# Hypermixer after linear attention: output columns written in token order with one store a tile, and one pool of eight PSUM banks

## The chip, the cores and the metric

The kernel runs on one core of one Trainium2 chip. The metric is the device time of the whole program in microseconds (us), lower is better. Before the change it took 134.56 us (median of three runs, 133.71 to 135.49). Each kernel also has one execution under the hardware profiler; "span" is the length of that execution, about 1.8 us shorter than the time the same run is booked with. On one core a run is called slow when it is over 1.5% above the fastest run of the same kernel.

Engines in the profile: PE is TensorE's matmul, PEld its weight load, DVE VectorE, ACT ScalarE, POOL GpSimd, SP SyncE, which issues most of the DMAs. A name with q (SPq, ACTq) is that engine's instruction queue.

## The reference, cut to what matters

```python
# attention: q, k, v are (8 batches, 8 heads, 576 tokens, 64), fp32
q_p = phi(q); k_p = phi(k)              # relu, times cos and sin of the position
kv  = einsum('bhsf,bhsd->bhfd', k_p, v); z = sum(k_p, axis=2)
attn = (q_p @ kv) / (q_p . z + 1e-6)
x = attn as (8, 576, 512)
# hypermixer: token mixing whose weights are made from x itself
wq = x @ w_q; wk = x @ w_k              # 512 -> 64
W  = einsum('bsd,btd->bst', wq, wk) / 8
mixed = einsum('bst,btd->bsd', W, x)
out = relu(mixed) @ w_out               # (8, 576, 512) fp32
```

The kernel never forms W: it computes kx = wk^T x (64 x 512) and then mixed^T = kx^T wq^T. 28.3 MB of q, k and v come in and 9.44 MB go out.

## The kernel before

A sequence of 576 tokens is cut as token = 9 p + c, with p from 0 to 63 and c from 0 to 8. On the chip a batch's tokens stand in the order (c, p), so a run of 64 columns holds tokens 9 apart. `mix_sb` holds relu(mixed)^T for two batches, bf16, 512 features on partitions (four groups of 128) by 2 x 576 token columns. Its columns are the weights of the last matmul, so their order is the order of the output's rows.

```python
CS = ((0, 5), (5, C9))                 # C9 = 9;  hs = 288, S = 576, D = 64
K0, N0, M0, M1, M2, M3 = 0, 2, 4, 5, 6, 7    # PSUM banks: qT and kv own 0-1, num owns 2-3

def mx_mm(b, j, m):                    # mixed^T: half the columns, two groups of features
    nh, i = divmod(j, 2)
    for r in range(2):
        rhs = (wT_bufs[b % 2][0:64, D + nh * hs:D + (nh + 1) * hs] if r == 0
               else wqTs[b][64:128, nh * hs:(nh + 1) * hs])
        nc.tensor.matmul(bank(m + r)[:, 0, 0:hs],
                         kxs[b][half_rows(r), i * P:(i + 1) * P], rhs, start=True, stop=True)

def mx_evac(b, j, m, eng):             # PSUM fp32 -> SBUF bf16, with relu and scale
    ...
    c0 = (b % 2) * S + nh * hs
    dst = mixs[b // 2].rearrange("p (r i) n -> p r i n", r=2)[:, :, i, c0:c0 + hs]
    src = bank(m, 2)[:, :, 0:hs]
    if eng is nc.scalar: nc.scalar.activation(dst, src, AF.Relu, scale=scale_moe)
    else: eng.tensor_scalar(dst, src, scale_moe, 0.0, op0=ALU.mult, op1=ALU.max)

def wout_mm(bp, rt, m):                # one output tile: 128 columns of mix_sb
    for dmc in range(NDM):
        nc.tensor.matmul(bank(m)[:, 0, :], mixs[bp][:, dmc, rt * P:(rt + 1) * P],
                         wo_sb[:, dmc, :], start=(dmc == 0), stop=(dmc == NDM - 1))

def store(bp, rt, qs):                 # two halves of 64 rows, 9 rows apart in DRAM
    for hi in range(2):
        qs[hi].dma_start(
            dataclasses.replace(out, offset=out.offset + out_dest(bp, rt, hi),
                                ap=[[C9 * DM, 64], [1, DM]]),
            o_sbs[bp, rt][64 * hi:64 * hi + 64, :])
```

A scheduler in the kernel (`plan_order`) fixes the order of all pieces and the engine of each evacuation beforehand. It simulates the engines with a table of times for each piece and picks the piece that can start first, less a weight for its priority. A half batch is called H (0 to 15). Names that occur below: qT, kv, num, norm, xT are attention's pieces for one H; wqk, wk, kx and mx make the mix for one batch; wo is an output tile. In the old scheduler mx, wo and the pieces before mx share banks 4 to 7.

## Time and profile before

| | before |
|---|---|
| time, median (range) | 134.56 us (133.71 to 135.49) |
| span of the profiled run, mean granted clock | 130.8 us, 0.974 |
| busy: PE, DVE, ACT, POOL | 105.8, 93.8, 78.5, 76.8 us |
| of PE's busy time, warm-up matmuls | 9.4 us |
| evacuation of mix: 24 on ACT, 8 on DVE | 657 and 756 ns each |
| last v cast; start of the last half batch's K-V product (kv.15) | 96.93; 105.15 us |

The two groups that the change touches most, from the table of the costliest groups. The columns are line, engine, operation, output and input with shapes and types, count; then busy us in all and mean ns of one; then the engine's idle time just before them and what ended it:

```profile
L520 ACT ACTIVATE mix_sb<-ps 128x576 bf16<-128x576 f32 x24 | 14.7, 657 | 2.4 <-PE ps L508 2.4
...
L522 DVE TENSOR_SCALAR mix_sb<-ps 128x576 bf16<-128x576 f32 x8 | 6.0, 756 | 4.0 <-PE ps L508 4.0
```

### The profile page before, as it was taken

To read this page: it belongs to the slowest core of one execution; us is meant where nothing else is said; L and a number is where in the kernel's file an instruction comes from. 1 tells how busy PE (TensorE), PEld (TensorE's weight loads), DVE (VectorE), ACT (ScalarE), POOL (GpSimd) and SP (SyncE) were. 2 spreads that over 40 slices of the span, in tenths; PEclk is the share of its full clock that TensorE was granted. 3 is DMA by queue.
4 is the path that set the end of the run, shared out by engine and by line. 5 is a ranking of instruction groups with operands and counts; after the bars stand their busy time and mean duration, and the time that the engine had idled before them with its cause. 6 is when DMAs were issued, how large, how long until landed. Compare 5 with 4: busy or idle time off the path is not lost.

```text
span 130.8 us, 5363 instructions
## 1 busy us (share of the span) xinstructions
PE 105.8 (81%) x2279; PEld 61.8 (47%) x2279; DVE 93.8 (72%) x153; ACT 78.5 (60%) x154; POOL 76.8 (59%) x121
## 2 busy tenths in 40 slices
PE   5947685885699989986999699889947999899930
PEld 2325253563546546643756366556624664443300
DVE  1065979689994999959999987989659876346200
ACT  6950063658756796639557595787637865655440
POOL 7728988896779999975697876885371000000000
PEclk9999999999959999999999999999999999999995
DMA  3999999999999999999999999999974034837973
GB/s 88 369 383 394 345 310 403 394 388 390 389 393 388 374 391 396 401 378 376 316 393 413 368 359 378 383 373 295 382 214 87 5 80 89 177 75 167 211 226 110
DMA packets 21239, 39.40 MB, mean 301 GB/s; under 512 B 3040, under 2 KB 4576, under 8 KB 21216
## 3 DMA queue, kind: packets, MB, share of 16 engines
q1 hardware_dynamic: 20544, 38.08, 85.0%
q10 hardware_dynamic: 672, 0.98, 2.5%
q8 instruction: 18, 0.29, 0.9%
q14 instruction: 5, 0.04, 0.1%
HBM read 29.62 MB, written 9.44 MB: 299 GB/s over the span
## 4 chain that ended last, share of the span: by engine, by line
PE 43%; DMA 23%; DVE 14%; ACT 5%; POOL 5%; issue 4%; SPq 2%; ACTq 1%; POOLq 0%
PE ps L532 19%; DMA raw<-in_k_dram 12%; DMA raw<-in_q_dram 9%; PE ps L422 5%; PE ps L462 5%; PE ps L397 5%; DVE kp L361 4%; DVE qpt_buf L389 4%; PE ps L492 3%; POOL rk L348 3%; PE ps L447 2%; PE ps L383 2%; DVE x_sb L435 2%; PE ps L508 2%; POOL rq_buf L348 2%
## 5 line engine op out<-in xcount | busy, mean ns | idle before, releaser
L532 PE MATMUL ps<-wo_sb,mix_sb 128*128 128x512 bf16 x144 | 37.3, 386 | 2.0 <-issue 1.7
L348 POOL TENSOR_SCALAR rq_buf<-raw 128x640 bf16<-128x640 f32 (+1 forms) x32 | 26.2, 835 | 9.3 <-DMA raw<-in_q_dram 7.9
L373 POOL TENSOR_SCALAR v_buf<-raw 128x640 bf16<-128x640 f32 (+1 forms) x30 | 27.1, 920 | 7.4 <-DMA raw<-in_v_dram 6.6
L361 DVE TENSOR_TENSOR kp<-rk,cossin 128x2304 bf16<-128x2304 bf16 (+2 forms) x17 | 22.5, 1324 | 11.3 <-ACT rk L346 6.1
L335 ACT COPY o_sb<-ps 128x512 f32<-128x512 f32 x32 | 18.8, 586 | 15.8 <-PE ps L532 12.9
L435 DVE TENSOR_TENSOR x_sb<-ps,rec 128x640 bf16<-128x640 f32 x32 | 26.4, 824 | 1.1
L389 DVE TENSOR_TENSOR qpt_buf<-ps,cst 128x1152 bf16<-128x1152 bf16 x32 | 22.6, 747 | 0.0
L348 POOL TENSOR_SCALAR rk<-raw 128x640 bf16<-128x640 f32 (+1 forms) x30 | 19.5, 669 | 4.2 <-DMA raw<-in_k_dram 2.7
L422 PEld LDWEIGHTS <-qpt_buf 64*128 64x128 bf16 x640 | 14.3, 95 | 14.0 <-issue 13.2
L422 PE MATMUL ps<-kv_sb,qpt_buf 64*128 64x65 bf16 x320 | 16.3, 193 | 4.2 <-DVE x_sb L435 3.7
L532 PEld LDWEIGHTS <-mix_sb 128*128 128x128 bf16 x144 | 11.9, 98 | 15.6 <-issue 4.1
L335 ACT COPY xT_buf<-ps 128x640 bf16<-128x640 bf16 (+1 forms) x25 | 15.7, 650 | 3.0 <-PE ps L447 1.7
L422 PE MATMUL ps<-kv_sh,qpt_buf 64*128 64x65 bf16 x320 | 16.3, 192 | 1.1 <-issue 0.2
L397 PE MATMUL ps<-v_buf,kp 64*128 64x65 bf16 x576 | 13.1, 190 | 3.8 <-DVE qpt_buf L389 2.9
L520 ACT ACTIVATE mix_sb<-ps 128x576 bf16<-128x576 f32 x24 | 14.7, 657 | 2.4 <-PE ps L508 2.4
L397 PEld LDWEIGHTS <-kp 64*128 64x128 bf16 x576 | 10.6, 94 | 8.2 <-issue 3.4
L335 ACT CAST kv_sb<-ps 128x260 bf16<-128x260 f32 x13 | 4.9, 378 | 12.4 <-PE ps L397 12.2
L508 PE MATMUL ps<-wT_buf,kx 64*128 64x288 bf16 x32 | 8.5, 292 | 2.6 <-ACT mix_sb L520 1.9
L258 PE MATMUL ps<-warm 128*128 128x512 bf16 x31 | 9.4, 441 | 1.5 <-DVE warm L254 1.5
L383 PE MATMUL ps<-ident,rq_buf 64*128 64x64 bf16 x288 | 8.1, 192 | 2.6 <-POOL rq_buf L348 1.3
L433 DVE RECIPROCAL rec<-ps 128x10 f32<-128x10 f32 x32 | 6.8, 213 | 4.0 <-PE ps L426 3.8
L462 PE MATMUL ps<-xT_buf,wqk_sb 128*128 128x288 bf16 x64 | 9.2, 287 | 0.0
(51 smaller groups left out, 115.8 us busy)
## 6 DMA issues: line engine op xcount, KB each, us to landing
raw<-in_q_dram SPq DMA_DIRECT2D x15, 576.0 KB, 7.1
raw<-in_k_dram SPq DMA_DIRECT2D x15, 576.0 KB, 7.3
raw<-in_v_dram SPq DMA_DIRECT2D x15, 576.0 KB, 7.2
out_dram<-o_sb SPq DMA_DIRECT2D x67, 128.0 KB, 5.3
wo_f<-in_moe_w_out_dram SPq DMA_DIRECT2D x1, 1024.0 KB, 10.2
out_dram<-o_sb ACTq DMA_DIRECT2D x5, 128.0 KB, 2.9
raw<-in_k_dram ACTq DMA_DIRECT2D x1, 320.0 KB, 4.5
raw<-in_q_dram SPq DMA_DIRECT2D x1, 320.0 KB, 4.2
```

What stands on the lines that cost most here:

```text
L335: nc.scalar.copy(dst, src)
L348: eng.tensor_scalar(dst, src, FMAX, 0.0, op0=ALU.min, op1=ALU.max)
L361: nc.vector.tensor_mul(kp[H][:, 2 * lo:2 * hi], rks[H][:, lo:hi].rearrange("p c i d -> p (c i) d").unsqueeze(2) .to_broadcast([P, 2 * (hi ...
L373: eng.tensor_scalar(dst, src, 1.0, 1.0, op0=ALU.mult, op1=ALU.mult)
L389: nc.vector.tensor_mul(qpt_bufs[H % 2][:, r, :, D:SLOTS * D], bank_h(K0 + r)[:, 0:1, 0:HC].to_broadcast([P, 2, HC]), cst)
L397: nc.tensor.matmul(bank(K0 + r)[:, 0, i * (D + 1):(i + 1) * (D + 1)], kp[H][half_rows(r), 2 * c + i, :, :], v_bufs[H % 3][half_rows(r), c, ...
L422: nc.tensor.matmul(nb[t][:, u, :], qpt_bufs[H % 2][rows, r, w, u * P:(u + 1) * P], mv, start=(u == 0 and w == 0), stop=False)
L435: nc.vector.tensor_tensor(xv[:, h, r], nv[:, :, :, 0:D], rec.to_broadcast([P, 2, SC, D]), op=ALU.mult)
L462: nc.tensor.matmul(bank(m + nh)[:, 0, 0:hs], wqk_sb[:, dmc, :, :], xT_bufs[b % 2][:, dmc, nh * hs:(nh + 1) * hs], start=(dmc == 0), stop=( ...
L508: nc.tensor.matmul(bank(m + r)[:, 0, 0:hs], kxs[b][half_rows(r), i * P:(i + 1) * P], rhs, start=True, stop=True)
L520: nc.scalar.activation(dst, src, AF.Relu, scale=scale_moe)
L532: nc.tensor.matmul(bank(m)[:, 0, :], mixs[bp][:, dmc, rt * P:(rt + 1) * P], wo_sb[:, dmc, :], start=(dmc == 0), stop=(dmc == NDM - 1))
```

## The change

The intent is fourfold. Output tiles become 128 consecutive rows, so one store over 128 partitions replaces two over 64. For that, the evacuation of the mix writes each column to its token's place. The scheduler gives all eight PSUM banks to all pieces from one pool instead of reserving four of them. And its table of times is replaced by one said to come from a trace. The core of the diff:

```diff
 def mx_mm(b, j, m):
     nh, i = divmod(j, 2)
+    lo, hi = CS[nh]                    # halves of 320 and 256 columns, whole values of c
     ...
 def mx_evac(b, j, m, eng):
-        c0 = (b % 2) * S + nh * hs
-        dst = mixs[b // 2].rearrange("p (r i) n -> p r i n", r=2)[:, :, i, c0:c0 + hs]
-        src = bank(m, 2)[:, :, 0:hs]
+        c0 = (b % 2) * S
+        dst = (mixs[b // 2].rearrange("p (r i) n -> p r i n", r=2)[:, :, i, c0:c0 + S]
+               .rearrange("p r (s c) -> p r c s", c=C9)[:, :, lo:hi, :])
+        src = (bank(m, 2)[:, :, 0:(hi - lo) * D]
+               .rearrange("p r (c s) -> p r c s", c=hi - lo))
     ...
-    def store(bp, rt, qs):
-        for hi in range(2):
-            qs[hi].dma_start(...)      # as above
+    rows = out.rearrange("b s d -> (b s) d")
+    def store(bp, rt, eng):
+        r0 = 2 * bp * S + P * rt
+        eng.dma_start(rows[r0:r0 + P, :], o_sbs[bp, rt])
     ...
     # plan_order: times, priorities, dependencies, and banks
-        op(("qT", H), {"PE": .27}, [ago(H, "rq", H), ago(H, "kve", H - 1)], pa, "row")
+        op(("qT", H), {"PE": .26}, [ago(H, "rq", H), ago(H, "kv", H - 1),
+                                    ago(H > 1, "num", H - 2, 1)], pa, "row", 2)
-            op(("mxe", b, j), {"ACT": .67, "DVE": .76}, [("mx", b, j)], par["pme"], ...)
+            op(("mxe", b, j), {"ACT": .56, "DVE": .71}, [("mx", b, j)], par["pme"], ...)
-                        u = min((0, 2), key=lambda i: max(bank[i], bank[i + 1]))
+                        u = min((0, 2, 4, 6), key=lambda i: max(bank[i], bank[i + 1]))
     ... # likewise kv, num, norm, xT, wqk, kx, wo; a model of fetch pauses on PE
```

In the new `dst` the innermost index is p, and one step of it is 9 bf16 elements, 18 bytes.

## The prediction

> **What bounds the kernel now**
>
> I read the page's slices first, then busy time by stage, the waits, what the DMA engines moved in two short stretches, and the end of the chain of waits. From the slices (3.27 us each; busy in tenths):
>
> ```profile
> PE   5947685885699989986999699889947999899930
> DMA  3999999999999999999999999999974034837973
> GB/s 88 369 383 394 345 310 403 394 388 390 389 393 388 374 391 396 401 378 376 316 393 413 368 359 378 383 373 295 382 214 87 5 80 89 177 75 167 211 226 110
> ```
>
> The DMA engines are full until 98 us and then nearly idle, while PE works on to 125.5. So there are two limits in a row: inputs until 98 us, then whatever PE has not done yet. The table by stage puts numbers on it (columns: length, busy time of each engine, granted clock, DMA share, GB/s):
>
> ```profile
> 7.00:20.00 13.00, 8.93 (x216) 5.12 (x217) 9.60 (x17) 3.69 (x9) 9.56 (x12) 1.00 1.06 359
> 20.00:34.00 14.00, 9.57 (x304) 6.80 (x305) 12.19 (x20) 8.52 (x19) 11.45 (x16) 1.00 1.05 393
> 34.00:50.00 16.00, 14.73 (x318) 8.72 (x310) 13.73 (x21) 11.07 (x25) 14.52 (x20) 0.89 1.05 387
> 50.00:66.00 16.00, 14.29 (x351) 9.04 (x351) 13.90 (x24) 9.71 (x19) 12.30 (x15) 1.00 1.03 373
> 66.00:82.00 16.00, 14.59 (x367) 8.89 (x366) 14.32 (x25) 11.01 (x22) 12.45 (x18) 1.00 1.03 381
> 82.00:98.00 16.00, 13.37 (x340) 8.42 (x337) 12.68 (x22) 10.93 (x25) 10.82 (x14) 1.00 0.95 330
> 98.00:105.15 7.15, 6.02 (x166) 3.97 (x162) 6.44 (x12) 5.19 (x11) 0.71 (x2) 1.00 0.20 43
> 105.15:125.50 20.35, 19.46 (x223) 9.07 (x222) 9.80 (x18) 11.97 (x22) 0.00 (x0) 1.00 0.64 142
> 125.50:130.80 5.30, 0.00 (x0) 0.00 (x0) 0.00 (x0) 0.69 (x2) 0.00 (x0) 0.69 0.52 154
> ```
>
> I cut at 105.15 because there the K-V product of the last half batch (kv.15) starts. POOL casts its v from 96.93 to 98.71, so the input was ready 6.4 us before PE came to it. Then PE is 96% busy for 20.35 us, and 5.3 us follow the last matmul. So the end is: when PE reaches kv.15, plus 20.35, plus 5.3. From 34 us to kv.15 PE is idle 71.15 - (14.73 + 14.29 + 14.59 + 13.37 + 6.02) = 8.15 us, and from 7 to 34 us 27 - 18.50 = 8.5 us. That idle time is what a new schedule can win. The waits name it:
>
> ```profile
> PE ps L422 <- DVE x_sb L435: 3.7, 6, 1.1
> PE ps L397 <- DVE qpt_buf L389: 2.9, 8, 0.5
> PE ps L508 <- ACT mix_sb L520: 1.9, 4, 1.1
> PE ps L532 <- issue: 1.7, 1, 1.7
> ```
>
> Three of the four are waits for a PSUM bank: num for the norm that empties banks 2-3, kv for the q evacuation that empties banks 0-1, mx for an evacuation in the pool of four. Together 8.5 us over the run, 4.9 of it before 34 us.
>
> **What the Trainium skill says**
>
> "SBUF — State Buffer", section "Door 1: The DMA port swizzle": DMA bandwidth depends on how many of the 16 SBUF ports the partitions reach, and 64 consecutive partitions reach 8. The kernel stores each output tile as two halves of 64 partitions. The trace agrees. Loads alone at 24-38 us run at 391 GB/s. Around 62-64 us, where two tiles' halves are in the queue, the rate drops to 150-292 while the engines stay busy, and in the drain from 120 to 126 us, with stores alone, it is 214:
>
> ```profile
> DMA packets 2547, 5.47 MB, mean 391 GB/s; under 512 B 132, under 2 KB 132, under 8 KB 2544
> ...
> DMA packets 780, 1.28 MB, mean 214 GB/s; under 512 B 161, under 2 KB 161, under 8 KB 779
> ```
>
> "Runtime: NRT & Kernel Launch", section "Instruction fetch mechanics": instructions come in 16 KiB blocks of 256, and the cost is "mostly hidden". The trace has 18 packets and 0.29 MB on the instruction queue, which fits the block size; hidden is only partly true: PE's one long "issue" wait, 1.7 us before 97.1, has no other releaser, and I take it for a fetch behind the full queue.
>
> "VectorE: DVE Perf Modes", section "Why PSUM operands drop a tier": an fp32 PSUM operand caps the op at 1×, so the mix evacuation has no fast mode to lose by a strided output. The trace agrees: 756 ns for 576 elements. The SBUF page's note on 16-byte cachelines in the same Door 1 section says bf16 can stride for free up to 8 elements; the new writes step by 9 elements (18 bytes). No run here shows yet what that costs.
>
> **The change, part by part**
>
> *Stores.* The mix evacuation now writes columns in token order, so an output tile is 128 consecutive rows and 36 stores of 256 KB over 128 partitions replace 72 of 128 KB over 64. Bytes stay. What the half rate cost before the last load: from 34 to 98 us the four stages fall 3, 17, 9 and 60 GB/s short of 390, which is 16 x (3 + 17 + 9 + 60)/390 = 3.65 us. About 1.3 of that is the stretch 96.5-98 where no load is left, so 2.4 us. The order of DMA issues also puts 17 instead of 18 tiles ahead of the last v load: 0.26 MB / 390 GB/s = 0.7 us. The last v is cast about 3 us earlier, at 95.7 instead of 98.7. This is permission for PE, not yet gain. It also halves SP's store issues (0.547 us each, 36 fewer) and the number of DMAs in flight that must retire before the next issue.
>
> *Banks.* qT, kv and num no longer own fixed pairs. In the new order kv.0 stands before the q evacuation, and kv.15 no longer needs qe.15 out of its banks. On DVE, qe.14 and both norms of 13 now stand before mk.15; before, they stood behind it, so H = 14 hung back to kv.14 at 99.92. Before 34 us I expect 1.5 of the 4.9 us of bank waits back (the rest is data that is not there yet, and the output weights' 1 MB now load two halves earlier, ahead of q.3). Between 34 us and kv.15 I expect 3.5 of the 8.15 us back. So kv.15 moves from 105.15 to about 100.2, 4.4 us after its input is ready: PE's own work is then the limit, not the inputs.
>
> *PE work.* The same: 36 output tiles (144 matmuls at 386 ns), 32 num, 32 mx. I counted the new order after kv.15: 13 output tiles, as before. So the 20.35 us stay, except that kx.6 and kx.7 now have their evacuations (372 ns, with semaphores about 0.5 us) uncovered before mx.6.0 and mx.7.0: +1.0 us. The 12 more warm-up matmuls (30 against 18 beside the opening 13) stand in gaps and cost nothing.
>
> *The end.* The chain of waits for the last tiles:
>
> ```profile
> 121.35 2.36 DMA out_dram<-o_sb
> ...
> 123.81 0.59 ACT o_sb L335
> ...
> 125.63 0.47 ACTq L542
> ...
> 126.20 0.58 ACT o_sb L335
> ```
>
> ACT issues half of every late store between two evacuations: 0.59 + 0.47 and gaps, about 1.2 us a tile against PE's 0.97. It also waits for an output buffer that a slow store holds. The last evacuation so starts at 126.20, 0.7 us after its matmul. Now ACT issues only tiles 5 and 7 and stores drain at twice the rate: I take off 0.7 us here and 0.5 us of the 4.0 us from the last evacuation to the end.
>
> *Sum.* -1.5 - 3.5 + 1.0 - 1.2 = -5.2 us: a span of 125.6. The profiled span is 130.8 where the median time is 134.56; in the same ratio that is 134.56 x 125.6/130.8 = 129.2. Because PE at this density meets fetch stalls that I cannot place, I add 0.4: 129.6 us.
>
> **Rivals**
>
> *PE stays late.* PE has about 96 us of its own work (105.8 busy less 9.4 warm-up). If the idle time is mostly fetch and dependencies rather than banks, it moves and does not shrink. For it: the 1.7 us issue wait, and more instructions than before (4584 rows against 4560). Then only the end and about 1.5 us come off: 132 us.
>
> *The strided write costs.* If an 18-byte step adds a third to 32 mix evacuations (ACT 657 ns, DVE 756), that is 0.23 x 32 = 7 us spread over two engines at 60 and 72% busy, of which the last four lie before the final tiles: +0.5 us at the end. Against it: the scheduler's new table, said to come from a trace, lowers these ops (0.67 to 0.56, 0.76 to 0.71). The answer would still be about 130.
>
> *DVE takes over.* It is busy 14.32 of 16 us at 66-82, and something holds POOL up (its q casts of 640 elements average 904 ns, its k casts of the same shape 718). If the inputs come 3 us sooner, DVE could be the next bound. The moves of work are small (mix evacuations 13 on DVE instead of 8, output ones 0 instead of 4, K-V ones 1 instead of 3), so nothing much is relieved: 131.
>
> *The full gain.* Were PE to keep right behind the inputs, kv.15 would start at 96.5: about 126.
>
> **Range and chances**
>
> Centre 129.6. The slow rivals give 131-132.5, the full gain 126-127: the 8-in-10 range is 126.4 to 132.4. Faster by over 2% means under 131.9: 0.80. Within 2%: 0.17. Slower, which would need a schedule that fails outright: 0.03.
>
> **What would show it**
>
> Right: store stretches in the body without dips to 200 GB/s; the last v cast near 95-96 us; kv.15 near 100; PE's waits for norm and q evacuations well under 6.6 us together; about 21 us from kv.15 to the last matmul; the last evacuation directly behind it. Wrong: mix evacuations longer than 0.66/0.76 us; kv.15 still 6 us behind its input; issue waits of several us on PE; or a stretch from kv.15 to the end that has grown by more than 1 us.

## The result, and the profile after

| | before | after |
|---|---|---|
| time, median (range) | 134.18 us (133.71 to 135.49) | 175.0 us (173.0 to 175.32) |
| span, mean granted clock | 130.8 us, 0.974 | 173.6 us, 0.848 |
| busy: PE, DVE, ACT, POOL | 105.8, 93.8, 78.5, 76.8 | 117.1, 117.4, 117.2, 73.6 |

Four runs of each in the same rounds. The ratio is 1.299, with a 95% interval of 1.285 to 1.313. A ratio here is the mean time of one kernel's fast runs over that of the other's fast runs of the same rounds, so it is not quite the ratio of the medians. The change made the kernel 30% slower. The prediction had 129.6 us and gave "slower" three chances in a hundred.

The slices of the changed kernel (4.34 us each) show the new shape at once:

```profile
PE   6686677369963368932897289918991883794790
DMA  4999999965999603998098908992741030053046
GB/s 152 376 391 344 363 391 393 392 236 160 332 342 396 247 4 93 355 344 342 7 316 259 338 20 260 380 391 94 223 158 64 0 127 0 25 216 126 0 181 242
```

Before, the DMA row was solid nines until the loads were done. Now it breaks off again and again, down to 4 and 7 GB/s, and PE has holes at the same rhythm. Something stops everything at once, several times. The shares of the chain that ended last say what, by engine and then by line:

```profile
PE 41%; ACT 27%; DMA 12%; DVE 8%; issue 6%; POOL 3%; ACTq 0%; DVEq 0%; POOLq 0%
ACT mix_sb L551 22%; PE ps L561 21%; DMA raw<-in_k_dram 5%; DMA raw<-in_v_dram 5%; PE ps L489 4%; PE ps L449 4%; PE ps L424 4%; DVE mix_sb L553 3%; DMA raw<-in_q_dram 2%; PE ps L519 2%; PE ps L410 2%; ACT o_sb L362 2%; PE ps L536 2%; ACT kv_sh L362 2%; DVE kp L388 2%
```

The evacuations of the mix, L551 and L553, are 22 + 3 = 25% of the chain, which is 43 us of 173.6. The group rows that answer to the two shown before:

```profile
L551 ACT ACTIVATE mix_sb<-ps 128x512 bf16<-128x512 f32 (+1 forms) x19 | 50.1, 2859 | 2.7 <-PE ps L536 2.6
...
L553 DVE TENSOR_SCALAR mix_sb<-ps 128x640 bf16<-128x640 f32 (+1 forms) x13 | 34.5, 2832 | 6.4 <-PE ps L536 5.9
```

One of them takes 2.86 us where it took 0.66, and 2.83 where it took 0.76, for the same number of elements overall. PE's waits, as who waits, for whom, us in all, how often, the longest:

```profile
PE ps L449 <- ACT mix_sb L551: 10.9, 6, 2.7
PE ps L474 <- DVE mix_sb L553: 9.6, 4, 2.6
PE ps L536 <- ACT mix_sb L551: 6.8, 3, 2.8
PE ps L561 <- ACT mix_sb L551: 4.2, 3, 2.7
```

L449 is num and L474 is xT: pieces of attention that now take banks from the common pool and wait for a bank that holds a mix tile being emptied. L536 is mx itself and L561 the output matmul. The stop then reaches the inputs. SP issues loads and stores in one order, and a store waits for its output evacuation. Before:

```profile
SPq L542 <- ACT o_sb L335: 11.2, 11, 4.4
```

After:

```profile
SPq L571 <- ACT o_sb L362: 104.1, 33, 13.6
```

SP stands 104.1 us in such waits, up to 13.6 at a time, and the loads that stand behind the store don't start: POOL waits 37.6 us for loads of q, k and v to arrive, where it waited 17.2. The last v is cast at 126.52 us instead of 96.93; its own last wait, 5.3 us, is for PE, so the late inputs and the late PE hold each other up. PE runs at a lower granted clock as well (0.848): an output matmul takes 462 ns instead of 386.

### The profile page after: what moved, and what is told of

It is laid out like the page before. It is cut to its first block, busy times and chain, and to the rows that moved or that the text cites. A ratio compares the mean times of both kernels' runs of the same rounds, so it can differ in the third digit from the quotient of the medians.

```text
span 173.6 us, 5340 instructions
## 1 busy us (share of the span) xinstructions
PE 117.1 (67%) x2269; PEld 70.5 (41%) x2291; DVE 117.4 (68%) x148; ACT 117.2 (68%) x159; POOL 73.6 (42%) x121
## 3 DMA queue, kind: packets, MB, share of 16 engines
HBM read 29.62 MB, written 9.44 MB: 225 GB/s over the span
## 4 chain that ended last, share of the span: by engine, by line
PE 41%; ACT 27%; DMA 12%; DVE 8%; issue 6%; POOL 3%; ACTq 0%; DVEq 0%; POOLq 0%
ACT mix_sb L551 22%; PE ps L561 21%; DMA raw<-in_k_dram 5%; DMA raw<-in_v_dram 5%; PE ps L489 4%; PE ps L449 4%; PE ps L424 4%; DVE mix_sb L553 3%; DMA raw<-in_q_dram 2%; PE ps L519 2%; PE ps L410 2%; ACT o_sb L362 2%; PE ps L536 2%; ACT kv_sh L362 2%; DVE kp L388 2%
## 5 line engine op out<-in xcount | busy, mean ns | idle before, releaser
L551 ACT ACTIVATE mix_sb<-ps 128x512 bf16<-128x512 f32 (+1 forms) x19 | 50.1, 2859 | 2.7 <-PE ps L536 2.6
L561 PE MATMUL ps<-wo_sb,mix_sb 128*128 128x512 bf16 x128 | 42.5, 462 | 6.7 <-ACT mix_sb L551 4.2
L553 DVE TENSOR_SCALAR mix_sb<-ps 128x640 bf16<-128x640 f32 (+1 forms) x13 | 34.5, 2832 | 6.4 <-PE ps L536 5.9
L362 ACT COPY o_sb<-ps 128x512 f32<-128x512 f32 x36 | 21.3, 591 | 24.5 <-PE ps L561 23.9
L449 PE MATMUL ps<-kv_sb,qpt_buf 64*128 64x65 bf16 x320 | 16.6, 207 | 12.9 <-ACT mix_sb L551 10.9
L561 PEld LDWEIGHTS <-mix_sb 128*128 128x128 bf16 x144 | 14.8, 114 | 24.2 <-issue 16.5
L449 PEld LDWEIGHTS <-qpt_buf 64*128 64x128 bf16 x640 | 14.9, 105 | 17.2 <-issue 16.7
L449 PE MATMUL ps<-kv_sh,qpt_buf 64*128 64x65 bf16 x320 | 16.7, 208 | 0.2
L362 ACT COPY xT_buf<-ps 128x512 bf16<-128x512 bf16 (+1 forms) x24 | 16.2, 729 | 0.1
L474 PE MATMUL ps<-ident,x_sb 64*128 64x64 bf16 x288 | 8.3, 199 | 11.4 <-DVE mix_sb L553 9.6
L536 PE MATMUL ps<-wT_buf,kx 64*128 64x320 bf16 (+1 forms) x32 | 6.6, 291 | 11.1 <-ACT mix_sb L551 6.8
L285 PE MATMUL ps<-warm 128*128 128x512 bf16 x37 | 12.0, 453 | 2.2 <-DVE warm L281 1.5
L474 PEld LDWEIGHTS <-x_sb 64*128 64x128 bf16 x288 | 6.8, 100 | 14.3 <-issue 12.0
```

Of the source, the lines that this page charges most:

```text
L362: nc.scalar.copy(dst, src)
L449: nc.tensor.matmul(nb[t][:, u, :], qpt_bufs[H % 2][rows, r, w, u * P:(u + 1) * P], mv, start=(u == 0 and w == 0), stop=False)
L474: nc.tensor.transpose(bank_h(m + r)[:, 0, k0 * D:(k0 + 1) * D], xs[b][half_rows(r), u, 2 * hp:2 * hp + 2, :], ident[half_rows(r), half_row ...
```

## The experiments

The question was first which part of the change costs 41 us, and then why the rest of it gains so little. Theory one: the 18-byte step of the writes makes the evacuation slow, and all else follows. Its rival: the pool of eight banks, or the new order, lets any evacuation stop attention, and the slow write only adds to it. A second rival: the new stores.

Twelve kernels ran, in three calls of four. The kernel before ran beside each; its median was 134.43 us in the first, 134.57 in the second and 133.22 in the third. In the second (e5 to e8) only one of its four runs was fast, at 131.54, so there is no ratio of fast runs for these, and I compare with what all four gave, 131.54 to 138.01. The profiles of e2, e4 and e12 fell on runs that count as slow, those of e6 to e11 on fast ones; what rests on the former alone is less sure. "e12", "e9" and so on are short for the labels.

### The writes alone, put back

```diff
# e12: the changed kernel with contiguous writes; the rows come out permuted
-        dst = (mixs[b // 2]...[:, :, i, c0:c0 + S]
-               .rearrange("p r (s c) -> p r c s", c=C9)[:, :, lo:hi, :])
-        src = (bank(m, 2)[:, :, 0:(hi - lo) * D]
-               .rearrange("p r (c s) -> p r c s", c=hi - lo))
+        dst = (mixs[b // 2].rearrange("p (r i) n -> p r i n", r=2)
+               [:, :, i, c0 + lo * D:c0 + hi * D])
+        src = bank(m, 2)[:, :, 0:(hi - lo) * D]
```

The result is wrong on purpose: the columns stay in the order (c, p), and the store writes them as if they were in token order. Everything else is the changed kernel, instruction for instruction.

> Wrong result on purpose (rows permuted): the changed kernel with nothing altered but the mix evacuation writing contiguous columns; the store stays one contiguous block of 128 rows. It takes the slow pattern of the store in the first experiment out. If the step of the mix writes is the whole loss: 131 to 134 us, as with runs of five or up to 2 us less. If the store also counts: above 140.

Measured: 132.13 us, ratio 0.987 (0.976 to 0.998) to the kernel before; two of its four runs were fast. The profiled run was a slow one, with a span of 131.0 us and a clock of 0.948. The evacuations by form, and PE's waits above 1 us except two, among all engines' waits:

```profile
L550 ACT ACTIVATE mix_sb<-ps 128x640 bf16<-128x640 f32 x9 | 6.3, 705 | 2.1 <-PE ps L536 2.1
...
L550 ACT ACTIVATE mix_sb<-ps 128x512 bf16<-128x512 f32 x10 | 5.9, 597 | 1.3 <-PE ps L536 1.3
...
L552 DVE TENSOR_SCALAR mix_sb<-ps 128x640 bf16<-128x640 f32 x7 | 5.8, 824 | 7.2 <-PE ps L536 6.7 <-ACT kv_sh L362 0.5
...
L552 DVE TENSOR_SCALAR mix_sb<-ps 128x512 bf16<-128x512 f32 x6 | 4.1, 680 | 0.0
```

```profile
PE ps L410 <- issue: 3.3, 2, 1.9
...
PE ps L424 <- POOL v_buf L400: 2.4, 2, 1.3
PE ps L410 <- POOL rq_buf L375: 2.0, 3, 1.0
...
PE ps L424 <- issue: 1.3, 1, 1.3
PE ps L474 <- issue: 1.1, 1, 1.1
```

173.6 - 131.0 = 42.6 us of span come from the write pattern alone; against the spans of e12's two fast runs, 128.5 and 129.6, it is 44 to 45. This settles the main question, and the second rival falls with it, since e12 keeps the new store. The durations fit: the 19 evacuations on ACT took 2859 - 649 = 2.21 us longer each, 42 us, and the 13 on DVE 2832 - 757 = 2.07 us each, 27 us. That is 69 us; neighbours overlap a little, so that busy time grew by 64 (50.1 + 34.5 against 11.5 + 9.4). They lie on two engines side by side, and 25% of the chain after against 5% here (3% on DVE, 2% on ACT) put about 37 us of them on the path. What else lies on the path shifts too: PE's share falls from about 80 to 71 us, DMA's rises from 13 to 21. The shares are rounded to whole per cent, so this supports the 42.6 and does not prove it.

The second fence is about the gain that was expected, and I come back to it.

### The writes alone, put into the old kernel

```diff
# e3: the kernel before, old scheduler and old banks, with
+ mx_mm in halves of 320 and 256, the token-order dst and src of the change,
+ the single contiguous store, and the four evacuations of a batch as a tile's dependencies
```

> The kernel before, with its old scheduler and fixed banks, and only the token-order mix writes and the single contiguous store put in (an output tile then waits for all four mix evacuations of its batches). Theory 1: mix evacuations of 2.4 to 3.0 us, so 32 x 2.1 = 67 us more work on two engines, time 155 to 175 us. Theory 2: 132 to 138 us.

Measured: 196.21 us, ratio 1.466 (1.454 to 1.478), above even the 155 to 175 that theory one expected. The old scheduler put 27 of the evacuations on ACT, at 2894 ns each, and 5 on DVE at 2757. The evacuation on ACT is 32% of the chain. So the pool of eight banks is not needed for the loss. With attention's banks reserved the same writes cost more, not less, probably since the old order puts more of them on one engine; no run separates that. With e12, where pool and order stay and the loss is gone, the rival falls.

### What the step costs, by itself

```diff
# e5: the kernel before; after all of its work, each line three times on ACT and on DVE
+ evacuate 512 fp32 columns of PSUM to SBUF,
+   bf16 with steps of 1, 2, 4, 8, 9, 16 elements, fp32 with steps of 1, 2, 4, 9,
+   bf16 in runs of 5 out of 9 and 2 out of 9, and bf16 step 9 from a bf16 SBUF source
```

> The kernel before, and after all its work a series of single evacuations of 512 fp32 elements per partition from PSUM, each three times, on VectorE and then on ScalarE: bf16 output at steps of 1, 2, 4, 8, 9 and 16 elements, fp32 output at steps of 1, 2, 4 and 9, bf16 in runs of 5 and of 2 elements, and bf16 at step 9 from SBUF. From the mix evacuations (2.44 us for 512, 3.00 us for 640) step 9 should cost about 2.4 us on both engines. If the cost comes with each new 16-byte line, it is small at steps 2 and 4, full from step 8 on, and fp32 at step 4 or 9 is as slow as bf16. If it comes with writes of 2 bytes that have no neighbour, it is there from step 2 on and fp32 is fast at every step.

Measured in one profiled run; the correct result was kept. Rows of the probe, costliest first. On ACT: step 9 from SBUF (L688); from PSUM, steps of 8, 9 and 4 (L670, L672, L668), runs of two (L686), fp32 at step 4 (L680), a step of 2 (L666), runs of five (L684) and a step of 1 (L664). L661 is DVE at step 9 from SBUF:

```profile
L688 ACT ACTIVATE scr<-sbs 128x512 bf16<-128x512 bf16 x3 | 7.3, 2435 | 0.1
L670 ACT ACTIVATE scr<-ps 128x512 bf16<-128x512 f32 x3 | 7.3, 2431 | 0.1
...
L672 ACT ACTIVATE scr<-ps 128x512 bf16<-128x512 f32 x3 | 7.2, 2402 | 0.1
...
L668 ACT ACTIVATE scr<-ps 128x512 bf16<-128x512 f32 x3 | 3.9, 1302 | 0.1
...
L661 DVE TENSOR_SCALAR scr<-sbs 128x512 bf16<-128x512 bf16 x3 | 3.9, 1287 | 0.1
...
L686 ACT ACTIVATE scr<-ps 128x512 bf16<-128x512 f32 x3 | 3.3, 1102 | 0.1
...
L680 ACT ACTIVATE scf<-ps 128x512 f32<-128x512 f32 x3 | 3.2, 1066 | 0.1
...
L666 ACT ACTIVATE scr<-ps 128x512 bf16<-128x512 f32 x3 | 2.2, 737 | 0.1
...
L684 ACT ACTIVATE scr<-ps 128x510 bf16<-128x510 f32 x3 | 2.0, 657 | 0.1
...
L664 ACT ACTIVATE scr<-ps 128x512 bf16<-128x512 f32 x3 | 1.8, 597 | 0.1
```

DVE agrees with ACT to within 20 ns at steps of 2, 4, 8, 9 and 16 (726, 1290, 2419, 2390 and 2292 ns). Steps of 8, 9 and 16 cost about the same, a step of 4 about half, a step of 2 little. That is roughly what one sees when the time goes with the number of 16-byte lines (those of the note that the prediction quotes) written to. At steps of 8 and up each of 512 elements has a line for itself: 2431/512 = 4.7 ns a line. At step 4 two share one: 1302/256 = 5.1 ns. With fp32 at step 4, one line an element, ACT takes 1066 ns, 2.1 ns a line, and at step 9 1077. The count of lines is not the whole of it: runs of two in nine are 256 runs, 18 bytes apart, so they write to at least as many lines as step 4 does, and took less, 1102 ns. Neither expectation had it exactly. In the kernel the step is 9, and alone on ACT a 640-column evacuation took 3.00 us, 4.7 ns a column. Why 2-byte writes cost twice what 4-byte ones do stays open. One probe bears on it: at step 9 from a bf16 source in SBUF, DVE needs 1287 ns, but ACT still 2435.

### The same rows with runs of five

```diff
# e4: the changed kernel, loops of the evacuation exchanged
-               .rearrange("p r (s c) -> p r c s", c=C9)[:, :, lo:hi, :])
+               .rearrange("p r (s c) -> p r s c", c=C9)[:, :, :, lo:hi])
-               .rearrange("p r (c s) -> p r c s", c=hi - lo))
+               .rearrange("p r (c s) -> p r s c", c=hi - lo))
```

The same elements go to the same places, but the innermost index is now c: five (or four) neighbours in SBUF, then a jump. It is the reading of PSUM that strides.

> The changed kernel whole, same tile and same values, but each mix evacuation walks tokens outside and the five or four columns inside: writes in runs of 4 or 5 neighbouring elements (8 or 10 bytes) and PSUM reads in steps of 256 bytes. If the cost is paid for every write that is not next to the one before, it falls to a fifth or a quarter of the excess: 0.66 + 2.2/4.5, about 1.15 us each, time 132 to 142 us. If it is paid for any access pattern that is not contiguous in read or write, it stays at 2.4 to 3 us and the time at 170 to 180.

Measured: correct, 133.36 us, ratio 0.996 (0.990 to 1.002). On ACT an evacuation takes 744 ns (512 columns) and 771 (640), on DVE 724 and 826:

```profile
L551 ACT ACTIVATE mix_sb<-ps 128x512 bf16<-128x512 f32 x10 | 7.3, 744 | 0.7 <-PE ps L536 0.7
...
L551 ACT ACTIVATE mix_sb<-ps 128x640 bf16<-128x640 f32 x9 | 6.9, 771 | 1.7 <-PE ps L536 1.7
```

Exchanging two loops takes the changed kernel from 175 to 133.4 us. It also shows that the token order as such costs little (0.996 against e12's 0.987, with intervals that overlap); the step of the innermost index does.

### The stores

```diff
# e2: the changed kernel with contiguous columns, and two stores of 64 rows as before
# e1: the same columns, and one store of both halves
+        d0, d1 = out_dest(bp, rt, 0), out_dest(bp, rt, 1)
+        eng.dma_start(dataclasses.replace(out, offset=out.offset + d0,
+                          ap=[[d1 - d0, 2], [C9 * DM, 64], [1, DM]]), o_sbs[bp, rt])
```

> As the run before, but each output tile leaves in the two half stores of 64 partitions that the kernel before has; so only scheduler and banks are left of the change. Theory 1: 127 to 133 us; what it is above the run with one store is the worth of the single store, which I expect to be 1 to 3 us. If single stores are worth nothing, the two are equal within 0.5 us.

Measured (e2): 133.61 us, ratio 0.991 (0.983 to 0.999). This is the scheduler and the banks alone. PE's waits for norms and q evacuations are gone, kv.15 starts at 107.19 us in a slow profile, and the single store shows no gain beyond that: e2 and e12 differ in the store alone, and their ratios, 0.991 and 0.987, are within each other's intervals. These intervals are wide enough that up to about 2 us could hide in them.

> The changed kernel with its scheduler and eight-bank pool kept, but the mix evacuation writes contiguous columns again; the output tile still leaves in one store of 128 partitions, whose rows go to two groups of every ninth row. Theory 1 (the 18-byte steps of the mix writes are the whole loss): mix evacuations back from 2.86 us to about 0.66 on ScalarE and 0.76 on VectorE, time 126 to 131 us. Theory 2 (the new order of operations or the shared banks lose by themselves): above 150 us, with the waits for banks still there. Theory 3 (the store or its row order matters): no change from 175.

Measured (e1): correct, 267.14 us, ratio 2.003 (1.985 to 2.022). All three theories missed. The evacuations were back at 595 to 825 ns, by form; the store was at fault. In a stretch of the drain (length, busy time of each engine, clock, DMA share, GB/s):

```profile
200.00:240.00 40.00, 0.00 (x0) 0.00 (x0) 0.00 (x0) 1.76 (x3) 0.00 (x0) 0.50 0.13 51
```

A share of 0.13 is 2 of 16 engines, and 9.44 MB at 51 GB/s is 185 us. The Trainium skill has this: "DMA: Bandwidth & Descriptors", section "Why a DMA increments its semaphore by 16 and not by 1", says that a DMA runs on the largest number of engines, up to 16, that divides the slowest dimension of both its access patterns. My pattern's slowest dimension was 2. The trace agrees with the page, and I hadn't looked there first. It was a fault of the experiment, not of the change; e12 does the same comparison without it.

### Where the expected gain went

With contiguous writes or runs of five the change gained 0.4 to 1.3% (e4, e2, e12; for e4 that is within the noise), where the prediction had 3.7%. In e12's waits the three bank waits of the kernel before (8.5 us) are gone or small: none for norm or q evacuations is listed, and 2.2 us, in short pieces, for mix evacuations. But "issue" waits on PE, which were 1.7 + 1.0 us, are 3.3 + 1.3 + 1.1, and waits for POOL's casts of the inputs came up, from 1.3 to 4.4 us (4.4 in the fast profile of e6 as well). Two readings: the inputs come late because the stores stand before them in SP's order; or PE is held by its own instruction stream. In e4 SP waits 59.6 us for output evacuations and the last v cast is at 102.05 us, so the first is plausible.

```diff
# e6: e4, each store put three loads later into SP's order
+        if n[0] == "st":
+            held.append((nl + 3, n, eng, m)); continue
# e7: the kernel before (old scheduler, old banks) with e4's writes and the single store
# e8: e4, each store issued by ScalarE right after its evacuation
```

> The changed kernel with runs of five, and each store put three loads later in the queue of the engine that issues both, so that a load does not stand behind a store whose tile is not ready. Theory A (loads held up behind stores are why banks and single stores gain nothing): the DMA engines stay full until about 95 us, the last v cast is at 95 to 97 instead of 102, and the time falls to 127 to 131 us. Theory B (PE's own work and its instruction fetches set the pace anyway): the v cast comes earlier, but the time stays at 132.5 to 134.

Measured (e6): 135.27 us against 134.57, no gain; its fast runs, 133.89 to 135.84, are above the one fast run of the kernel before. The last v cast came at 93.91 us, 8.1 us earlier than in e4, and kv.15 started at 107.54 all the same. PE's issue waits were 2.8 + 2.5 us and some small ones.

> The kernel before with its old scheduler and fixed banks, token order written in runs of four and five, one contiguous store a tile: the single store alone. If the half rate of the 64-partition stores held the loads up as I reckoned in the prediction, it gains 1.5 to 3 us: 131 to 133. If it only changes the drain, 133 to 135.

Measured (e7): 135.56 us against 134.57, no gain either; its fast runs were 134.12 to 136.00. The DMA engines moved 396, 401 and 402 GB/s in the three stretches from 34 to 82 us, where they moved 387, 373 and 381 before. In the timelines of POOL and PE (start, length, engine, line, what) of e7:

```profile
92.07 1.63 POOL L372 TENSOR_SCALAR v_buf<-raw 128x640 bf16<-128x640 f32 x2 [0.74 <-DMA raw<-in_v_dram]
...
107.64 0.73 PE L396 MATMUL ps<-v_buf,kp 64*128 64x65 bf16 x36
```

The last v is cast 4.9 us earlier than in the kernel before, and kv.15 starts 2.5 us later. So the store does what was predicted of it here, and more, and no gain comes of it: PE doesn't use the permission.

> As the changed kernel with runs of five, but every store is issued by ScalarE directly behind its own evacuation, so the load queue holds loads only. Theory A: 127 to 131 us, with about 36 x 0.35 = 13 us of issue time more on ScalarE, which is busy 61%. Theory B: 132.5 to 135.

Measured (e8): 140.15 us against 134.57; its fastest run, 139.54, is above the slowest of the kernel before. The last v cast was at 96.78 us, but kv.15 only at 111.71. ScalarE now spent 36 issues of 0.34 us between its evacuations, and once waited 4.1 us (for a load of q, by the trace) with an evacuation that PE needed; PE waited 3.8 us for the mixer weights that ScalarE empties (wT). Both theories missed: in this kernel ScalarE, which others wait for, is the wrong engine for all the stores.

So it was not the inputs. Three more runs take the loads away.

```diff
# e9: e6, but only the first two half batches are loaded; wrong on purpose
+        if H > 1:
+            for nm in names: raw[nm, H] = raw[nm, H % 2]
+            return
# e10: as e9, but every load still runs, into a tile that nobody reads
+                nc.sync.dma_start(dummy, srcs[nm][b][:, h0:h0 + 2, :])
# e11: the kernel before with e9's edit
```

> Wrong result on purpose: the kernel with runs of five and stores three loads later, but only the first two half batches are loaded and all later ones reuse their data, so no input is ever late and the DMA engines carry little but stores. If PE's own order of work and its partners set the pace from 34 us on, the time falls only by what PE waited for inputs and at the start, about 5 us (128 to 131). If instruction fetches behind the full DMA queue are what stops PE, its issue waits of over 0.5 us (6 us between 34 and 108) vanish too and the time is 118 to 124.

> As the run before (wrong result on purpose), but the loads of the later half batches are still made, into tiles that nothing reads: inputs never late, DMA engines full until about 80 us. If fetches behind a full queue stop PE, the issue waits are back and the time is 4 to 8 us above the run without loads; if not, both are equal within 2 us.

Measured: e9 126.94 us, ratio 0.957 (0.950 to 0.963) to the kernel before, span 124.6, between the two ranges expected. e10 135.14 us, but only one of its four runs was fast, at 132.51 (span 130.7). Against the mean of e9's three fast runs, 126.76, that is 5.7 us; between the profiled spans, both of fast runs, it is 6.1; between the medians of all runs 8.2. In both no piece waits for inputs to arrive once the first two half batches are in (20 us), and the same instructions run on PE. The PE lines with "issue" in e10:

```profile
PE ps L417 <- issue: 2.6, 2, 1.8
...
PE ps L431 <- issue: 1.5, 1, 1.5
...
PE ps L481 <- issue: 1.0, 1, 1.0
```

They add to 5.1 us; e9 lists 0.2 in all. So a full DMA queue by itself, with no input late, makes PE pause in its own instruction stream, for most of the 6 us. PE's busy time is also 2.0 us longer in e10 (107.6 against 105.6), at a lower granted clock (0.959 against 0.982). What these pauses are shows in the kernel before. It has five pauses with "issue" of 0.2 us or more up to 97 us. I counted the weight loads of PE that ran before each of the last four; the second entry with an x is that count:

```profile
0.00:36.60 36.60, 25.41 (x607) 15.32 (x608) 25.31 (x40) 19.75 (x37) 27.61 (x59) 0.98 0.99 351
0.00:55.80 55.80, 43.76 (x991) 26.17 (x992) 42.13 (x66) 32.62 (x64) 46.14 (x83) 0.97 1.01 365
0.00:85.70 85.70, 70.06 (x1631) 42.25 (x1632) 68.48 (x111) 52.32 (x103) 68.43 (x110) 0.98 1.02 368
0.00:96.50 96.50, 79.42 (x1887) 48.29 (x1888) 76.05 (x123) 60.37 (x120) 75.01 (x119) 0.98 1.01 364
```

608, 992, 1632, 1888: the differences are 384, 640 and 256, each a multiple of 128. The first pause, which ends at 30.62 us, comes after 480, 128 less than 608. A weight load and its matmul are two instructions, so the pauses stand at multiples of 256 instructions, the block size that the page quoted in the prediction gives for instruction fetch. All five counts are 96 + 128 k, with a whole number k. In e6 five counts are within two of this form, and in e10, where the loads go into tiles that nobody reads, the pauses stand at 608, 735, 991 and 1119, within one. That they are fetches is inferred from this spacing and from e9 and e10; no row of the trace names them.

> The kernel before with only the first two half batches loaded (wrong result on purpose). It shows what the old order and fixed banks can do when no input is late. If the bank waits are a real limit there, it gains little, 3 to 6 us (128 to 131), and stays above the run of the new order with resident inputs by 4 us or more.

Measured (e11): 129.32 us, ratio 0.974 (0.966 to 0.982). The old order keeps its bank waits (3.5, 2.3 and 1.6 us) even when nothing is late. Fast runs of e9 are 2.3 us faster than those of e11 (0.957 against 0.974 of 133). That is all that the new order and banks gain where PE is not held up by fetches; I had expected at least 4. It includes whatever the single store, put later as in e6, does there.

## Why the prediction was wrong

**The step that failed** is the rival "the strided write costs", which sized the 18-byte step at a third more, "0.23 x 32 = 7 us spread over two engines", half a microsecond at the end. It measured 4.4 times the old duration on ACT (2859 ns against 657) and 3.7 times on DVE (2832 against 756): 69 us over two engines, and 42.6 us of span (e12). The prediction's first sign of being wrong, mix evacuations longer than 0.66 and 0.76 us, is what came. The same mistake in the main sum is the silent assumption that 32 evacuations keep their 0.66 and 0.76 us. Three things misled me. I read "no fast mode to lose" as "nothing to lose", though a cap on reading says nothing of writing. I took the scheduler's new table (0.67 to 0.56, 0.76 to 0.71) for a measurement of the new form; it fits the contiguous form of e12 (597 and 680 ns for 512 columns) far better than the new one. And I had the note on 16-byte lines in hand, which pointed at this very step, and gave it no size of its own. A probe like e5 costs one run.

**Banks.** That the bank waits go was right: the waits for norm, q and mix evacuations, 8.5 us, fall to 2.2 in e12. That this gives 3.5 us back before kv.15 was wrong even with contiguous writes. kv.15 starts at 106.59 in e12, 5.9 us after its input is ready, and at 107.54 in e6, not at 100.2. PE runs into the pauses, by inference instruction fetches, behind the full queue instead (e9 against e10), as the rival "PE stays late" said; that rival's 132 us is near what e12 measured (132.13, and 130.22 and 131.36 in its fast runs). All in all PE's idle time and warm-ups together are 130.8 - 96.4 = 34.4 us before and 131.0 - 93.2 = 37.8 in e12, so no idle time was won.

**Stores.** That stores of 64 partitions drain more slowly was read rightly: from 128 to 131 us e6's stores of 128 partitions move 335 GB/s, where those of 64 moved 214 from 120 to 126. "The last v is cast about 3 us earlier" held only under the old order: 4.9 us in e7. With the new order it came later, by 2.5 us in e12 (99.41) and by 30 in the changed kernel, where SP's loads stood behind the stores of late tiles; I had not considered that. With the stores put later, as in e6, it is early (93.91). "Permission for PE, not yet gain" was right: e6 and e7 gained nothing by it.

**PE's work and the end.** From kv.15 to the end of the last output matmul I counted 20.35 us plus 1.0 for kx. In e12 it is 126.99 - 106.59 = 20.4 us, with PE's waits for kx at 1.5 us instead of 0.5 as I said. The last evacuation stands directly behind its matmul in e12 (127.03), as predicted. So PE's part of the end was predicted 1 us too long, and its order was right; in the changed kernel it is hidden behind the rest.

**From span to time.** The sum scales a span of 125.6 by 134.56/130.8 to get 129.2. But the profiled run was itself booked with 132.56, 1.8 us above its span, so the same span would be booked with about 127.4. That error is small beside the 42.6 us.

**Range.** 0.03 for "slower" left no room for a mechanism that I had named, had a page for, and had not measured.

No version beat the kernel before by 2%. The best correct ones are the changed kernel with runs of five (0.996) and with contiguous columns and two stores (0.991), both within 2%.

## What to carry to other kernels

Look at the innermost step of what an engine writes, not only at what it reads: where output must be permuted, try, as e4 did, to let the innermost loop be the one that is contiguous in SBUF and the PSUM side stride. A table of times that comes with a change describes some form of the operation, not necessarily the new one, so time the new form alone first. And a wait taken away from PE under a full DMA queue is only a gain if nothing else, its own instruction stream included, is next in line: check that with the loads taken out, and again with dummy loads put in.

## What the Trainium skill lacked or had wrong

- "SBUF — State Buffer", the note on cachelines in "Door 1: The DMA port swizzle": it says that fp32 can be strided for free up to 4 elements and bf16 up to 8. For writes neither held: fp32 at step 4 took 1066 ns instead of 696 (ACT, 512 elements), bf16 at step 4 took 1302 and at step 8 2431 instead of 597. A step of 2 cost nothing with fp32 (619) and 140 ns with bf16 (737). The page gives no size for the penalty: where each element has a line for itself, about 4.7 ns an element with 2-byte writes and 2.1 ns with 4-byte ones, the same on ACT and DVE. The sizes that the skill does have for a stepped output, in "Vector Engine (DVE) Microarchitecture Reference", are for 4-byte elements on DVE; no page has them for 2-byte elements or for ACT.
- "VectorE: DVE Perf Modes", on PSUM operands: it says nothing of the output's step, which took one operation from 691 to 2390 ns. DVE at step 9 takes 1287 ns from a bf16 SBUF source and 2390 from fp32 PSUM; no page has this.
- "Runtime: NRT & Kernel Launch", on instruction fetch: the cost is called mostly hidden. Behind a full DMA queue it was not: 5.1 us of issue waits on PE in a span of 130.7, against 0.2 without the loads. That these are fetches is inferred.
